# Scores of the late chunks: two fp32 products per head become one stacked fp32r product

## The chip, the cores and the metric

The kernel runs on one core of a Trainium2 chip. The metric is the time of one execution on the device, in microseconds (us). Before the change the median of three runs is 931.97 us, the lowest 931.91 and the highest 932.5. The profile was taken from a further execution of 931.88 us, whose span from the first to the last instruction is 930.1 us.

## The reference, cut to what matters

Two batches of 8 heads with 768 positions of 40 channels go through a gated linear attention (the state of an mLSTM); its output, 1536 tokens of 320 channels, goes through a two-layer network of 2048 hidden channels and then through eight experts of 1024 hidden channels whose weights come from a balanced gate:

```python
C = f_stab[:, :, None, None] * C + i_stab[:, :, None, None] * np.einsum('bhd,bhe->bhde', vt, kt)
n = f_stab[:, :, None] * n + i_stab[:, :, None] * kt
h_tilde = np.einsum('bhde,bhe->bhd', C, qt)          # y = o * h_tilde / max(|n.q|, 1)
...
h = x @ w_in
g = np.maximum(0.01 * h, h)
return (g @ w_out).astype(np.float32)
...
for e in range(E):
    h = np.maximum(x @ w1[e], 0.0)
    out += P[:, e:e + 1] * (h @ w2[e])
```

The kernel computes the recurrence by chunks of 128 tokens. Inside a chunk the scores of a head are the 128 by 128 products of its keys and queries over 40 channels; they are multiplied by a matrix of decays and applied to the values, and a state (`Cst`) carries the rest from chunk to chunk.

## The kernel before, in words

There are 12 chunks. The chunks 0 to 5, and the first 32 steps of the first network (`TABLE = 32`), are issued in a hand-written order, the string `ORDER`, whose words name tasks (`c5.sc` is the scores of chunk 5). Behind the table a loop runs over the steps 32 to 98. A step of this network is `up` (eight matmuls `ha`, L223, 256 columns wide), `leak` and `inner_high` on ScalarE, `inner_low` (`hla`, L723, one subtraction on GpSimd or VectorE) and, three steps later, `down` (six matmuls `ya`, L230 to L232, 320 columns wide). When a run of steps is complete, `empty` adds the sum `ya` into `x` from PSUM (L746, VectorE) or copies it (ScalarE); the next run then reuses the PSUM tiles. Chunks 6 to 11 hang on the steps of this loop by the table of numbers `ATTEND`: the decays of a chunk, its `scores`, its `values`, `recall` and `state`, and its `turn` (the transposes that make `xT`). In the loop the framework's scheduler may interleave what stands in neighbouring tasks; each engine then runs its own instructions strictly in the order in which they are issued.

`scores` (L586 to L592) runs for each head one fp32 matmul with 40 rows of contraction, at partition 0 or 64 by turns. An fp32 matmul shows as two records in the trace, so a chunk has 16 records at L591. `weigh` (L597, VectorE, two instructions) multiplies the scores by the decays and so releases their PSUM tiles.

Other work stands around these places. `decay_mask` (L576) is one GpSimd instruction on 128x1024 numbers; `weigh_keys` (L602) another on 128x320; `spread` (L559, tile `bd`) one on 64x1024. `Cst` (L665) is updated by three VectorE instructions per chunk. The sums of float halves (L259 `rawU`, L315 `rawx`) prepare weights and tokens of the experts; the token turns of the experts (`x0[p].repeat`, `.turn`, `.sums`, steps 36, 54 and 58) copy `x` (L777, `rr`), transpose it on TensorE (L308, `px`) and sum it on VectorE (L315).

What the steps of the loop do in a row:

```python
for g in range(TABLE, NG + LAG):
    up(g); leak(g); inner_high(g); inner_low(g)
    for fn in before[g]: fn()
    down(g - LAG); empty(g - LAG)
    for fn in after[g]: fn()
```

Of the kernel before, what the change touches and what calls it, by code (L numbers as in the profile page):

```python
# [8 lines left out]
F32 = mybir.dt.float32  # L9
F32R = mybir.dt.float32r  # L10
# [4 lines left out]
ALU = mybir.AluOpType  # L15
# [5 lines left out]

ATTEND = ((0, 2, 6, 11, 14), (5, 6, 10, 11, 14), (0, 3, 6, 8, 14), (5, 7, 9, 12, 14))
RUNS = ((0, 0, 8), (1, 0, 12), (0, 8, 16), (1, 12, 16))
MASKED = (0, 1, 2, 3)
VECTORED = ('pl2', 'pl4', 'pu9', 'pu10', 'pu12', 'pl14', 'pl15')
# [18 lines left out]
d15 g17 pl14 h17 u18 pu14 l17 c5.sg pa12 u19 g18 h18 pl13 d16 pb12 g19 l18 d17 h19 l19 u20 pa14 u21 pa13 g20 ph12 pb13  # L46
d18 h20 g21 l20 d19 h21 pb14 ph15 u22 l21 e19 u23 g22 h22 ph13 d20 l22 wl px12 g23 d21 h23 ph14 l23 u24 px14 d22 g24 h24
u25 l24 px15 u26 g25 px13 d23 c5.ou g26 h25 h26 d24 l25 l26 f9 c5.tt@3 u27 c4.tt@1 g27 u28 h27 l27 f7 d25 g28 c5.cr
c4.xi u29 d26 c4.xl g29 h28 h29 d27 l28 l29 u30 e27 u31 g30 c5.xi h30 d28 ws c5.xl c6.bd g31 h31 l30 l31 c4.cr
"""  # L50

F64_SCALE = 2.0 ** -112
# [3 lines left out]
def mlstm_moe_kernel(ctx, tc, qp, q3, kp, kn, vn, gates_in, og, cst_in, scr_in, w_in, w_out, w_gate, w1, w2, out):  # L56
    nc = tc.nc
    B, NCH, P = qp.shape[0:3]
    S = NCH * P
    NT, DM = out.shape  # L60
    D = 40
    DV = D + 1
# [14 lines left out]
    HP = NQ // P  # L77
# [3 lines left out]
    wp = ctx.enter_context(tc.tile_pool(name="wp", bufs=1))  # L81
    x2p = ctx.enter_context(tc.tile_pool(name="x2p", bufs=1))
# [4 lines left out]
    R = B * 32  # L87
    R3 = R + 32
# [3 lines left out]
    bdm = cst[:, P:P + GV]  # L92
# [257 lines left out]
    x2s, X, RRB = {}, {}, [1]  # L350
# [4 lines left out]
    with ExitStack() as st1:  # L355
        ac = st1.enter_context(tc.tile_pool(name="ac", bufs=1))
# [9 lines left out]
        def view(*shape):  # L366
            n = 1
            for x in shape:
                n *= x
            t = R0[:, home[0]:home[0] + n]  # L370
            home[0] += n
            assert home[0] <= R0.shape[1]
            return t.rearrange("p (a b) -> p a b", a=shape[0]) if len(shape) > 1 else t

        sig0 = view(8, DM)
        places = {"kP": view(4, P), "qP": view(4, P), "vt": view(9, DV), "q3": view(G, P), "kn": view(8, D),
                  "Dm": view(8, P), "Pm": view(8, P), "yt": view(8, DV), "dm": view(G, GV)}
        kw = view(9, D)
        sc0 = ac.tile([R3, 2 * S + 512 + 9 * D], F32, tag="sc0", name="sc0")
        sc1 = x2p.tile([R3, 3, S], F32, tag="XT", name="sc1")  # L380
        Ft, It, rst = sc0[0:R, 0:S], sc0[0:R, S:2 * S], sc0[0:R, 2 * S:2 * S + 512]
        ex = sc0[:, 2 * S + 512:].rearrange("p (h d) -> p h d", d=D)
        Mt, G3, T1 = sc1[0:R, 0, :], sc1[:, 1, :], sc1[0:R, 2, :]
        Gt = G3[0:R]


        rawU = ac.tile([P, 7 * UW], F32, tag="rawU", name="rawU")
# [111 lines left out]
        class Chunk:  # L499
# [45 lines left out]
                    nc.sync.dma_start(self.k, kn[self.b, self.s0:self.s0 + P])  # L545

            def load(self):
                self.load_kP()
                self.load_qP()

            def load_rest(self):
                self.load_v()
# [140 lines left out]
        chunks = [Chunk(c) for c in range(NCK)]  # L693
# [40 lines left out]
        def empty(g):  # L734
            j, f = steps[g]
            if (j, f) not in lasts:
                return
            part = sig0[:, 2 * j % 8:2 * j % 8 + 2, :]
            q = 2 * j // (2 * HP)
            if f == NFA - 1 and q not in x2s:  # L740
                x2s[q] = (ac, x2p)[q].tile([P, 2 * HP, DM], F32, tag=("sc0", "XT")[q], name=f"x2_{q}")
            for t in range(2):
                y = yp[j][t]
                o = x2s[q][:, (2 * j + t) % (2 * HP), :] if f == NFA - 1 else part[:, t, :]
                if j in summed:
                    nc.vector.tensor_tensor(o, y, part[:, t, :], op=ALU.add)  # L746
                else:
                    nc.scalar.activation(o, y, AF.Copy)
            summed.add(j)


        before = {g: [] for g in range(NG + LAG)}
        after = {g: [] for g in range(NG + LAG)}
        def attend(c, g_decay, g_scores, g_values, _, g_turn):
            after[g_decay].append(c.decay)
            before[g_scores].append(c.scores)
            after[max(g_scores, g_decay)] += [c.weigh, lambda: c.weigh_keys(nc.gpsimd)]
            before[g_values] += [c.values, c.recall, c.state]
            after[g_values].append(c.attend_all)
            before[g_turn].append(c.turn)  # L760
            if c.ck + 1 < NCK:
                after[g_scores].append(chunks[c.ck + 1].load)
                after[g_values].append(chunks[c.ck + 1].load_rest)

        for j in range(3, NBA):
            g0 = (j - 1) * NFA
            a, b = chunks[2 * j], chunks[2 * j + 1]
            if j > 3:
                after[g0 - 1].insert(0, lambda a=a, b=b: a.spread(b, nc.gpsimd))
            attend(a, *[g0 + x for x in ATTEND[2]])  # L770
            attend(b, *[g0 + x for x in ATTEND[3]])
        after[2 * NFA + 2].append(lambda: load_og(8))
        after[2 * NFA + 8].append(lambda: sigmoid(8))
        g5 = (NBA - 1) * NFA
# [7 lines left out]
        x0, x1 = positions  # L782
        V, GP = nc.vector, nc.gpsimd

        for p, g in enumerate((36, 54, 58)):
            step(g - 1, x0[p].repeat, copy_rest)
            step(g, x0[p].turn, 0, ps_b)
            step(g + 1, x0[p].turn, 1, ps_b)
            step(g + 2, x0[p].sums, V, 0)
            step(g + 3, x0[p].sums, V, 1)  # L790
# [69 lines left out]
        def engine(name):  # L860
            return nc.gpsimd if name in POOLED else nc.vector
# [37 lines left out]
        with tc.manual_schedule():  # L899
            for _ in range(20):  # L900
                nc.tensor.matmul(wps, zero[:, 0:P], zero[:, 0:512], start=True, stop=True)
            for name in ORDER.split():
                name, _, home = name.partition("@")
# [31 lines left out]
    one = cp.tile([1, P], F32, tag="one", name="one")  # L935
# [232 lines left out]
    for it in range(8):  # L1168
        g = 4 + it // 2
# [141 lines left out]
```

## Time and profile before

| | |
|---|---|
| median of three runs | 931.97 us |
| profiled execution | 931.88 us |
| its span | 930.1 us |
| TensorE busy | 924.2 us, 99% |
| VectorE / ScalarE / GpSimd busy | 587.3 / 490.1 / 552.1 us |
| granted TensorE clock, mean | 0.999 |

The engines are called PE (TensorE), PEld (its weight loads), DVE (VectorE), ACT (ScalarE), POOL (GpSimd) and SP (the queue that issues DMAs). PE is busy nearly throughout, so an edit changes the time by what it takes from PE's stream or by what it makes PE wait. A row of the timeline gives start, busy time, engine, line, operation, and in brackets the idle time of that engine before it with what ended it. Records of PE overlap: a matmul's own duration is longer than its distance to the next one, and the distance is what it costs.

### The profile page before, as it was taken

The numbers are of one execution on the slowest core, as the hardware profiler recorded it, in microseconds if no ns is written. First come the engines' busy times: TensorE is split into PE (matmuls) and PEld (weight loads), VectorE is DVE, ScalarE is ACT, GpSimd is POOL, SyncE is SP. The second block draws the span as 40 slices with busy tenths as digits, with TensorE's granted clock in tenths as the row PEclk, the third lists the DMA queues.
The fourth block names the chain that finished last, engine by engine and source line by source line (L and its number), as shares of the span: only waits on it lengthen the run. The fifth ranks groups of instructions, "written<-read, shape, count | busy, mean of one in ns | idle before, by whom it ended". The sixth has DMA issues, their size and how long they took to land.

```text
span 930.1 us, 16892 instructions
## 1 busy us (share of the span) xinstructions
PE 924.2 (99%) x6192; PEld 903.2 (97%) x6192; DVE 587.3 (63%) x1180; ACT 490.1 (53%) x959; POOL 552.1 (59%) x574
## 2 busy tenths in 40 slices
PE   9999999999999999999999999999999999999998
PEld 5899999999999999999999999999999999999998
DVE  8998751523958587666656665665666565666655
ACT  6877445345763645555445445544544455454442
POOL 3330244443442756767777777777777777767762
PEclk9999999999999999999999999999999999999999
DMA  8773131110301110111111111111111111111002
GB/s 273 253 233 129 34 111 31 56 39 3 88 14 33 52 38 24 52 38 38 37 38 53 46 52 38 37 38 38 50 48 50 41 38 38 38 49 49 30 2 85
DMA packets 57384, 56.49 MB, mean 61 GB/s; under 512 B 7654, under 2 KB 48086, under 8 KB 57302
## 3 DMA queue, kind: packets, MB, share of 16 engines
q1 hardware_dynamic: 57302, 55.43, 19.7%
q8 instruction: 48, 0.79, 0.4%
q14 instruction: 34, 0.28, 0.1%
HBM read 53.43 MB, written 1.97 MB: 60 GB/s over the span
## 4 chain that ended last, share of the span: by engine, by line
PE 94%; DVE 3%; ACT 1%; DMA 1%; issue 1%; SPq 0%; ACTq 0%; DVEq 0%
PE y L230 12%; PE y L231 12%; PE y L232 12%; PE ha L223 9%; PE b L1030 8%; PE b L1031 8%; PE b L1033 8%; PE b L1032 8%; PE ya L230 3%; PE ya L232 3%; PE ya L231 3%; PE yps L607 2%; PE sps L591 1%; PE zps L613 1%; PE dps L619 1%
## 5 line engine op out<-in xcount | busy, mean ns | idle before, releaser
L1054 POOL TENSOR_TENSOR hl<-c,hh 128x384 fp32r<-128x384 f32 x192 | 197.3, 1028 | 180.2 <-ACT c L1053 155.5
L230 PE MATMUL y<-w_e,hh 128*128 128x320 f32 x768 | 238.6, 311 | 0.0
L231 PE MATMUL y<-w_e,hh 128*128 128x320 f32 x768 | 237.0, 309 | 0.0
L232 PE MATMUL y<-w_e,hl 128*128 128x320 f32 x768 | 236.9, 308 | 0.0
L1112 DVE SCALAR_TENSOR_TENSOR acc<-y,Pg,acc 128x320 f32<-128x320 f32 x336 | 179.1, 548 | 63.4 <-PE y L232 56.3
L1052 ACT ACTIVATE hh<-c 128x384 fp32r<-128x384 f32 x192 | 99.8, 520 | 208.5 <-DVE c L1049 208.5
L1030 PE MATMUL b<-X,w_e 128*128 128x384 f32 x448 | 152.7, 341 | 0.2 <-DVE s L1070 0.2
L1031 PE MATMUL b<-X,w_e 128*128 128x384 f32 x448 | 151.0, 337 | 0.0
L1033 PE MATMUL b<-X,w_e 96*128 96x384 f32 x448 | 151.0, 337 | 0.0
L1032 PE MATMUL b<-X,w_e 128*128 128x384 f32 x448 | 150.9, 337 | 0.0
L230 PEld LDWEIGHTS y<-w_e,hh 128*128 128x128 f32 x768 | 144.3, 188 | 1.7 <-DVE acc L1110 1.1
L231 PEld LDWEIGHTS y<-w_e,hh 128*128 128x128 f32 x768 | 144.3, 188 | 0.0
L232 PEld LDWEIGHTS y<-w_e,hl 128*128 128x128 f32 x768 | 144.2, 188 | 0.0
L1053 ACT ACTIVATE c<-c 128x384 f32<-128x384 f32 x192 | 101.0, 526 | 18.0 <-ACT hh L1052 0.7
L1049 DVE TENSOR_TENSOR c<-b,s 128x384 f32<-128x384 f32 x192 | 100.6, 550 | 13.4 <-PE b L1033 10.0
L223 PE MATMUL ha<-xT,w_a 128*128 128x256 f32 x768 | 107.8, 285 | 0.0
L223 PEld LDWEIGHTS ha<-xT,w_a 128*128 128x128 f32 x768 | 100.1, 190 | 1.1 <-ACT gg L712 0.2
L1077 DVE SCALAR_TENSOR_TENSOR hl<-b,hh 128x384 fp32r<-128x384 f32 x64 | 35.6, 557 | 95.4 <-ACT hh L1076 95.4
L723 POOL TENSOR_TENSOR hla<-gg,hha 128x256 fp32r<-128x256 f32 x64 | 49.3, 772 | 70.3 <-ACT hha L718 62.4
L259 POOL TENSOR_TENSOR raw_e<-raw_e 128x256 f32<-128x256 f32 x116 | 85.2, 743 | 4.5
L1030 PEld LDWEIGHTS b<-X,w_e 128*128 128x128 f32 x448 | 84.8, 189 | 1.3 <-DVE s L1070 0.6
L1031 PEld LDWEIGHTS b<-X,w_e 128*128 128x128 f32 x448 | 85.3, 190 | 0.0
(200 smaller groups left out, 1496.7 us busy)
## 6 DMA issues: line engine op xcount, KB each, us to landing
raw_e<-in_w_dram SPq DMA_DIRECT2D x31, 320.0 KB, 2.9
raw_e<-in_w_dram SPq DMA_DIRECT2D x62, 128.0 KB, 2.2
raw_e<-in_w_dram SPq DMA_DIRECT2D x248, 32.0 KB, 1.9
raws<-in_w_in_dram SPq DMA_DIRECT2D x8, 768.0 KB, 5.9
rawU<-in_w_out_dram SPq DMA_DIRECT2D x4, 640.0 KB, 5.6
R<-in_kp_dram SPq DMA_DIRECT2D x10, 256.0 KB, 3.4
R<-in_qp_dram SPq DMA_DIRECT2D x10, 256.0 KB, 3.6
raws<-in_w_out_dram SPq DMA_DIRECT2D x4, 640.0 KB, 4.6
```

The lines of the kernel that those rows point to most:

```text
L223: nc.tensor.matmul(h_ps, t1[:, ws, c * P:(c + 1) * P], xt[:, xs, t0:t0 + n], start=(j == 0), stop=(j == len(MM1) - 1),)
L230: nc.tensor.matmul(y_ps, a, t2[:, c, :], start=first, stop=False)
L231: nc.tensor.matmul(y_ps, a, t2[:, 2 + c, :], start=False, stop=False)
L232: nc.tensor.matmul(y_ps, b, t2[:, c, :], start=False, stop=last)
L1030: nc.tensor.matmul(bank, f[:, 0], b[:, 0], start=fresh, stop=False, skip_group_check=not fresh)
L1031: nc.tensor.matmul(bank, f[:, 0], b[:, 2], start=False, stop=False, skip_group_check=not fresh)
L1032: nc.tensor.matmul(bank, f[:, 2], b[:, 0], start=False, stop=False, skip_group_check=not fresh)
L1033: nc.tensor.matmul(bank, f[0:K3, 1], b[0:K3, 1], start=False, stop=True, skip_group_check=not fresh)
L1049: nc.vector.tensor_tensor(c, part, plus, op=ALU.add)
L1053: nc.scalar.activation(c, c, AF.Relu)
L1054: nc.gpsimd.tensor_tensor(hl[a][b], c, hh[a][b].bitcast(F32), op=ALU.subtract)
L1112: nc.vector.scalar_tensor_tensor(out=o, in0=y, scalar=Pg[:, 2 * HP * q + t, e:e + 1], in1=o, op0=ALU.mult, op1=ALU.add)
```

## The change: what it does

For chunks 6 to 11 `load` now brings each 40-row block of keys and queries three times, one under the other, into 120 partitions (six DMAs in place of two per chunk). `stack(n)` turns the keys (n = 0) and the queries (n = 1) of a chunk into a stack of fp32r numbers: for each half of the heads a CAST writes the rounded part of 120x512 numbers, and a SCALAR_TENSOR_TENSOR with two inputs in SBUF (the rounded part and the plain numbers) writes either the rounded part or the remainder, by a column of zeros and ones. These are eight new VectorE instructions per chunk. `scores_stacked` then runs one fp32r matmul per head, 120 rows deep, which sums the three products of rounded parts and remainders.

The stacks live in two of the three `raw` buffers until the scores of chunk 11. So the token turns 1 and 2 of expert 0, which need such buffers, stand at steps 72 and 74 in place of 54 and 58. The table's end gets the loads and both stacks of chunk 6. Two rows and one column of `ATTEND` that nothing reads are dropped.

```diff
-g31 h31 l30 l31 c4.cr
+g31 h31 l30 l31 c4.cr c6.ld c6.s0 c6.s1
...
             def load(self):
-                self.load_kP()
-                self.load_qP()
+                if self.ck == 10:
+                    second_half()
+                for t, src in zip(plain, (kp, qp)):
+                    src = src[self.b, self.c].rearrange("(i p) j t -> p i (j t)", i=2)[0:D]
+                    for r in range(3):
+                        nc.sync.dma_start(t[r * D:(r + 1) * D].rearrange("p (i m) -> p i m", i=2), src)
+
+            def stack(self, n):
+
+                if len(stacks) == n:
+                    stacks.append(wp.tile([GW, 12 * P], F32R, tag="raw", name=f"stack{n}", bufs=3))
+                t, x = stacks[n], plain[n]
+                one = bdm[0:GW, (n + 1) * DV:(n + 1) * DV + 1]
+                for i in range(2):
+                    s = slice(4 * i * P, 4 * (i + 1) * P)
+                    high = t[:, 8 * P:12 * P]
+                    nc.vector.tensor_copy(high, x[:, s])
+                    nc.vector.scalar_tensor_tensor(out=t[:, s], in0=high.bitcast(F32), scalar=one, in1=x[:, s],
+                                                   op0=ALU.mult, op1=ALU.subtract)
+
+            def scores_stacked(self):
+                self.sps = self.bank("sc")
+                for i in range(2):
+                    for j in range(4):
+                        t = slice((4 * i + j) * P, (4 * i + j + 1) * P)
+                        nc.tensor.matmul(self.sps[i][:, j, :], stacks[0][:, t], stacks[1][:, t], start=True, stop=True)
...
-        def attend(c, g_decay, g_scores, g_values, _, g_turn):
+        def attend(c, g_decay, g_scores, g_values, g_turn):
             after[g_decay].append(c.decay)
-            before[g_scores].append(c.scores)
+            before[g_scores].append(c.scores_stacked)
...
             if c.ck + 1 < NCK:
-                after[g_scores].append(chunks[c.ck + 1].load)
-                after[g_values].append(chunks[c.ck + 1].load_rest)
+                n = chunks[c.ck + 1]
+                after[g_scores].append(lambda: n.stack(0))
+                after[g_scores + 1].append(lambda: n.stack(1))
+                after[g_values].append(n.load_rest)
+            if c.ck + 2 < NCK:
+                after[g_scores + 1].append(chunks[c.ck + 2].load)
...
-        for p, g in enumerate((36, 54, 58)):
+        for p, g in enumerate((36, 72, 74)):
...
-        chunks[6].load()
         chunks[6].load_rest()
+        chunks[7].load()
```

The order in which VectorE works at chunk 6's scores, before the change (`x_0<-ya_12` is the sum that releases the PSUM tiles for the next run, `sps_6` the scores):

```order
L663 TENSOR_TENSOR R_76<-dps_668,cst 120x369
L259 TENSOR_TENSOR rawU<-rawU 128x256
L665 SCALAR_TENSOR_TENSOR Cst_106<-Cst_106,decC,R_76 120x123 x3
L259 TENSOR_TENSOR rawU<-rawU 128x256
L746 TENSOR_TENSOR x_0_1361<-ya_12_0_1378,R_76 128x320
L746 TENSOR_TENSOR x_0_1361<-ya_12_1_1379,R_76 128x320
L597 TENSOR_TENSOR R_76<-sps_6_1497,R_76 128x4x128
L597 TENSOR_TENSOR R_76<-sps_6_1498,R_76 128x4x128
```

And the same place in the changed kernel, from the update of `Cst` on:

```order
L699 SCALAR_TENSOR_TENSOR Cst_106<-Cst_106,decC,R_76 120x123 x3
L574 CAST stack_1409<-sc_96 120x512
L259 TENSOR_TENSOR rawU<-rawU 128x256
L575 SCALAR_TENSOR_TENSOR stack_1409<-stack_1409,cst,sc_96 120x512
L259 TENSOR_TENSOR rawU<-rawU 128x256
L574 CAST stack_1409<-sc_96 120x512
L259 TENSOR_TENSOR rawU<-rawU 128x256
L575 SCALAR_TENSOR_TENSOR stack_1409<-stack_1409,cst,sc_96 120x512
L574 CAST stack_1414<-R_76 120x512
L780 TENSOR_TENSOR x_0_1361<-ya_12_0_1378,R_76 128x320
L575 SCALAR_TENSOR_TENSOR stack_1414<-stack_1414,cst,R_76 120x512
L780 TENSOR_TENSOR x_0_1361<-ya_12_1_1379,R_76 128x320
```

Eight instructions now stand between the last update of `Cst` and the first sum into `x_0`, where one stood; three sums of `rawU` moved behind `Cst` (the other two stood some rows further up), and the second half of the queries' stack follows behind these rows.

TensorE at the same place in the changed kernel (`ya_0` are the PSUM tiles that the sums into `x_0` release; before, all eight score matmuls stood between the first and the second row, and the eight `ha` of one step were together):

```order
L223 MATMUL ha_1502<-xT_1318,w_a_415 128x256 x8
L230 MATMUL ya_0_0_1527<-w_a_302,hha_1440 128x320
L231 MATMUL ya_0_0_1527<-w_a_302,hha_1440 128x320
L232 MATMUL ya_0_0_1527<-w_a_302,hla_1441 128x320
L223 MATMUL ha_1545<-xT_1318,w_a_555 128x256
L583 MATMUL sps_6_1517<-stack_1414,stack_1409 128x128 x4
L230 MATMUL ya_0_1_1528<-w_a_302,hha_1440 128x320
L231 MATMUL ya_0_1_1528<-w_a_302,hha_1440 128x320
L232 MATMUL ya_0_1_1528<-w_a_302,hla_1441 128x320
L223 MATMUL ha_1545<-xT_1318,w_a_555 128x256 x4
L583 MATMUL sps_6_1518<-stack_1414,stack_1409 128x128 x4
```

The scores are split into two halves of four, and half the sums `ya` moved ahead of each.

VectorE between the weighing of chunk 6 and the scores of chunk 7 in the changed kernel (`rr_1` and `rawx_0` are the token turn at step 36, `zps`, `yps` and `dps` chunk 6's values, recall and state):

```order
L631 TENSOR_TENSOR R_76<-sps_6_1518,R_76 128x4x128
L574 CAST stack_1409<-sc_96 120x512
L575 SCALAR_TENSOR_TENSOR stack_1409<-stack_1409,cst,sc_96 120x512
L574 CAST stack_1409<-sc_96 120x512
L575 SCALAR_TENSOR_TENSOR stack_1409<-stack_1409,cst,sc_96 120x512
L815 COPY rr_1_2686<-x_0_1361 128x256 x2
L315 TENSOR_TENSOR rawx_0_1576<-rawx_0_1576 128x256 x4
L658 TENSOR_TENSOR R_76<-zps_1641,decT 128x328
L574 CAST stack_1414<-R_76 120x512
L663 TENSOR_TENSOR R_76<-yps_1632,R_76 128x328
L575 SCALAR_TENSOR_TENSOR stack_1414<-stack_1414,cst,R_76 120x512
L668 TENSOR_SCALAR den_1657<-R_76 128x8
```

The keys' stack of chunk 7 stands ahead of the copies and the queries' stack among chunk 6's values, and the four sums of `rawx` now follow one another; behind these rows come the second half of the queries' stack, the updates of `Cst` and the weighing of chunk 7.

## Rows read from the trace of the kernel before

**Rows 1.** The page: busy time and share of the span; the chain that ended last.

```profile
PE 924.2 (99%) x6192; PEld 903.2 (97%) x6192; DVE 587.3 (63%) x1180; ACT 490.1 (53%) x959; POOL 552.1 (59%) x574
...
PE 94%; DVE 3%; ACT 1%; DMA 1%; issue 1%; SPq 0%; ACTq 0%; DVEq 0%
```

**Rows 2.** Timeline of PE around chunk 11's scores: start us, busy us, then the instruction.

```profile
208.17 1.12 PE L223 MATMUL ha<-xT,w_a 128*128 128x256 f32 x8
209.22 1.16 PE L591 MATMUL sps<-R 40*128 40x128 f32 x16
...
210.56 0.31 PE L231 MATMUL ya<-w_a,hha 128*128 128x320 f32 x1
...
211.29 1.12 PE L223 MATMUL ha<-xT,w_a 128*128 128x256 f32 x8
212.25 0.31 PE L230 MATMUL ya<-w_a,hha 128*128 128x320 f32 x1
212.40 0.31 PE L231 MATMUL ya<-w_a,hha 128*128 128x320 f32 x1
```

**Rows 3.** Groups by line and shape, 95 to 225 us: count, busy us, mean ns.

```profile
L607 PE MATMUL yps<-R 128*128 128x41 f32 x96 | 11.4, 278 | 0.1
...
L441 DVE SCALAR_TENSOR_TENSOR mv<-mv,rco,sc 64x384 f32<-64x384 f32 x1 | 0.6, 599 | 0.0
```

**Rows 4.** Timeline of PE at the scores of chunks 6 and 7.

```profile
113.35 1.12 PE L223 MATMUL ha<-xT,w_a 128*128 128x256 f32 x8
...
122.63 1.87 PE L607 MATMUL yps<-R 128*128 128x41 f32 x16
...
127.90 0.94 PE L591 MATMUL sps<-R 40*128 40x128 f32 x12
```

**Rows 5.** Timeline of DVE in the same stretch.

```profile
109.28 0.41 DVE L259 TENSOR_TENSOR rawU<-rawU 128x256 f32<-128x256 f32 x1
109.61 1.73 DVE L665 SCALAR_TENSOR_TENSOR Cst<-Cst,decC,R 120x123 f32<-120x123 f32 x3
111.26 0.41 DVE L259 TENSOR_TENSOR rawU<-rawU 128x256 f32<-128x256 f32 x1
113.11 0.93 DVE L746 TENSOR_TENSOR x<-ya,R 128x320 f32<-128x320 f32 x2 [1.44 <-PE ya L232]
...
121.69 0.49 DVE L777 COPY rr<-x 128x256 f32<-128x256 f32 x2 [4.74 <-PE px L308]
125.53 0.50 DVE L624 TENSOR_TENSOR R<-zps,decT 128x328 f32<-128x328 f32 x1 [3.34 <-PE zps L613]
```

**Rows 6.** Timeline of POOL in the same stretch.

```profile
110.04 1.17 POOL L576 TENSOR_SCALAR_AFFINE_SELECT R<-R 128x1024 f32<-128x1024 f32 x1 [42.60 <-PE ha L223]
111.17 1.10 POOL L723 TENSOR_TENSOR hla<-gg,hha 128x256 fp32r<-128x256 f32 x1
112.23 0.74 POOL L602 TENSOR_TENSOR R<-R 128x320 f32<-128x320 f32 x1
112.93 1.44 POOL L723 TENSOR_TENSOR hla<-gg,hha 128x256 fp32r<-128x256 f32 x2
115.41 0.73 POOL L723 TENSOR_TENSOR hla<-gg,hha 128x256 fp32r<-128x256 f32 x1 [1.04 <-ACT hha L718]
122.39 0.73 POOL L723 TENSOR_TENSOR hla<-gg,hha 128x256 fp32r<-128x256 f32 x1 [6.25 <-ACT hha L718]
123.08 1.89 POOL L559 TENSOR_TENSOR bd<-mv,rco 64x1024 fp32r<-64x1024 f32 x1
...
125.98 1.32 POOL L576 TENSOR_SCALAR_AFFINE_SELECT R<-R 128x1024 f32<-128x1024 f32 x1
```

**Rows 7.** Two lines by themselves, whole span: ns shortest/median/longest.

```profile
L665 DVE SCALAR_TENSOR_TENSOR Cst<-Cst,decC,R x24: 294/342/1212, 34.5 to 178.8; 120x123 f32<-120x123 f32 x24
...
L777 DVE COPY rr<-x x10: 281/284/662, 105.3 to 254.5; 128x256 f32<-128x256 f32 x10
```

**Rows 8.** Windows: PE, PEld, DVE, ACT, POOL busy us, PEclk, DMA share, GB/s.

```profile
140.00:222.00 82.00, 82.00 (x666) 80.59 (x665) 23.90 (x60) 36.03 (x86) 34.52 (x44) 1.00 0.12 36
```

More of the change, by code (lines that the diff above doesn't have):

```diff
@@ L19 @@
 NEG = -1.0e30
-ATTEND = ((0, 2, 6, 11, 14), (5, 6, 10, 11, 14), (0, 3, 6, 8, 14), (5, 7, 9, 12, 14))
+ATTEND = ((0, 3, 6, 14), (5, 7, 9, 14))
 RUNS = ((0, 0, 8), (1, 0, 12), (0, 8, 16), (1, 12, 16))
@@ L48 @@
 u25 l24 px15 u26 g25 px13 d23 c5.ou g26 h25 h26 d24 l25 l26 f9 c5.tt@3 u27 c4.tt@1 g27 u28 h27 l27 f7 d25 g28 c5.cr
-c4.xi u29 d26 c4.xl g29 h28 h29 d27 l28 l29 u30 e27 u31 g30 c5.xi h30 d28 ws c5.xl c6.bd g31 h31 l30 l31 c4.cr
+c4.xi u29 d26 c4.xl g29 h28 h29 d27 l28 l29 u30 e27 u31 g30 c5.xi h30 d28 ws c5.xl c6.bd g31 h31 l30 l31 c4.cr c6.ld c6.s0 c6.s1
 """
@@ L375, in mlstm_moe_kernel @@
         sig0 = view(8, DM)
-        places = {"kP": view(4, P), "qP": view(4, P), "vt": view(9, DV), "q3": view(G, P), "kn": view(8, D),
+        both = view(8, P)
+        places = {"kP": both[:, 0:4], "qP": both[:, 4:8], "vt": view(9, DV), "q3": view(G, P), "kn": view(8, D),
                   "Dm": view(8, P), "Pm": view(8, P), "yt": view(8, DV), "dm": view(G, GV)}
@@ L379, in mlstm_moe_kernel, with second_half @@
         sc0 = ac.tile([R3, 2 * S + 512 + 9 * D], F32, tag="sc0", name="sc0")
-        sc1 = x2p.tile([R3, 3, S], F32, tag="XT", name="sc1")
+        sc1 = x2p.tile([P, 3, S], F32, tag="XT", name="sc1")
         Ft, It, rst = sc0[0:R, 0:S], sc0[0:R, S:2 * S], sc0[0:R, 2 * S:2 * S + 512]
         ex = sc0[:, 2 * S + 512:].rearrange("p (h d) -> p h d", d=D)
-        Mt, G3, T1 = sc1[0:R, 0, :], sc1[:, 1, :], sc1[0:R, 2, :]
+        Mt, G3, T1 = sc1[0:R, 0, :], sc1[0:R3, 1, :], sc1[0:R, 2, :]
         Gt = G3[0:R]
+        plain = [sc1.rearrange("p a s -> p (a s)")[0:GW, 0:8 * P], both[0:GW].rearrange("p h t -> p (h t)")]
+        stacks = []
+        def second_half():
+            t = x2p.tile([P, 3 * S], F32, tag="XT", name="x2_1")
+            x2s[1] = t[:, 0:2 * HP * DM].rearrange("p (t d) -> p t d", d=DM)
+            o = (2 * HP - 2) * DM
+            plain[0] = t[0:GW, o:o + 8 * P]
         rawU = ac.tile([P, 7 * UW], F32, tag="rawU", name="rawU")
@@ L740, in empty @@
             if f == NFA - 1 and q not in x2s:
-                x2s[q] = (ac, x2p)[q].tile([P, 2 * HP, DM], F32, tag=("sc0", "XT")[q], name=f"x2_{q}")
+                x2s[q] = ac.tile([P, 2 * HP, DM], F32, tag="sc0", name=f"x2_{q}")
             for t in range(2):
@@ L769, in mlstm_moe_kernel @@
                 after[g0 - 1].insert(0, lambda a=a, b=b: a.spread(b, nc.gpsimd))
-            attend(a, *[g0 + x for x in ATTEND[2]])
-            attend(b, *[g0 + x for x in ATTEND[3]])
+            for c, times in ((a, ATTEND[0]), (b, ATTEND[1])):
+                attend(c, *[g0 + x for x in times])
         after[2 * NFA + 2].append(lambda: load_og(8))
@@ L887, in mlstm_moe_kernel @@
         tasks["c6.bd"] = lambda: chunks[6].spread(chunks[7], engine("c6.bd"))
+        tasks["c6.ld"] = chunks[6].load
+        for n in range(2):
+            tasks[f"c6.s{n}"] = lambda n=n: chunks[6].stack(n)
         for n in range(2 * NUA):
```

## The prediction

> **What bounds the kernel now.** I read the page first, then PE's timeline where the edited matmuls stand, then the timelines of DVE and POOL beside them. PE is busy 924.2 of 930.1 us and makes 94% of the chain that ended last [rows 1], so the sum goes by PE: what leaves its stream is gained, and each time it waits is lost, since nothing later in the program stands still to absorb it. The reader should see in [rows 2] that a step without scores and one with scores differ by a whole block, and in [rows 5, 6] that DVE and POOL, though far from full, delay each other whenever they work side by side. The resolution that I use throughout is 0.2%, 1.9 us. The profiled execution took 931.88 us and the median is 931.97, so I sum against the former, and the 0.1 us between them is inside the rounding.
>
> **What PE's stream loses.** In a step without scores the second `ya` starts 1.11 us after the first `ha` (211.29 to 212.40); with chunk 11's scores it takes 2.39 us (208.17 to 210.56) [rows 2]. The scores cost 1.28 us per chunk. They become eight records. No row before shows an fp32r matmul with 128 columns, so I bound it. From below: `ha` has 256 columns and goes at 0.96/8 = 0.120 us each (211.29 to 212.25), `ya` 320 columns at 0.15 (212.25 to 212.40) [rows 2]; 0.027 to 0.03 us per 64 columns leads to about 0.063 us at 128, 0.50 per chunk, and 0.78 saved. From above: if fp32r at this width took two records as fp32 does, 16 records by the pitch of `yps`, (1.87 - 0.28)/15 = 0.106 us [rows 3, 4], make 1.70 us, and 0.42 is lost. The nearest row is `yps`: it streams only 41 columns per record and still cannot go faster than 0.106, and it loads 128 columns of 4-byte weights as the new matmul does. I take 0.11, so 0.88 per chunk. Saved: 0.40 per chunk, 2.4 us over six chunks; ends -4.7 and +2.5.
>
> The Trainium skill, "TensorE: Matmul & The Clock Gate", section "Back-to-back issue gap", gives 81 ns as the sustained distance of matmuls with their weight loads at 128 columns. By that figure the block would be 0.65 us and the saving 3.8 us, an estimate; no run here shows it.
>
> **What DVE gains, and what hides it.** Eight instructions per chunk come in. The scalar_tensor_tensor has no row at 512 columns: 384 columns took 0.60 us [rows 3] and 123 take 0.34 [rows 7], so 0.73 at 512, some 0.66 between starts. The cast lies between the copy of 256 columns (0.28, [rows 7]), which gives 0.35 at best, and the other instruction's 0.66; I take 0.40. A chunk's stacks are 4 x 0.66 + 4 x 0.40 = 4.2 us, 25 us for all. From 140 to 222 us DVE is busy 23.9 of 82 and PE never idle [rows 8]; chunks 8 to 11 put in about 17 us, and the moved token turns (two, by the same rows two copies, four sums each, some 5 us with waits) fall there too. That cover is wide, so I cost both at nothing; if a stack still came late, it would cost that chunk its 0.4 us gain first. The extra DMAs (four more per chunk on SP) for chunks 8 to 11 are issued a whole chunk ahead; for chunk 6 they stand before `rawU`'s loads, whose sums have moved later as well. The two tight places are chunk 6 and chunk 7.
>
> **The lock.** Three `Cst` updates with both inputs in SBUF took 1.73 us from 109.61, where three medians are 1.03; the longest single one is 1.21 us [rows 5, 7]. It ran beside POOL's affine_select of 110.04 to 111.21 and ended 0.13 us after that, so of its own 0.34 us 0.2 lay under POOL's end. POOL's next `hla` then took 1.10 us to 112.27 instead of the 0.72 to 0.74 of the others [rows 6]: its own 0.73 starts at 111.54, 0.13 before DVE's sum of 111.26 was over [rows 5]. By turns, each waits for nearly the whole instruction of the other. The sums that read PSUM (113.11, 0.93 for two) ran beside POOL's `hla` of 112.93 and neither lost anything. A copy too goes from 0.28 up to 0.66 [rows 7].
>
> The Trainium skill, "SBUF — State Buffer", section "Who interferes with whom", says that a DVE instruction with two SBUF inputs, or a copy or cast in a two-port mode, and a GpSimd instruction that reads SBUF exclude one another for the full instruction. The rows just read agree, at 1.21 us against 0.34. It is the rule that speaks against this change, because all eight new instructions are of these two kinds.
>
> **Chunk 6.** PE wants `ya_0` when its eight `ha` of 113.35 are through, at 113.35 + 0.96 = 114.31 [rows 2, 4]. That tile is free only after the sum `x_0<-ya_12_0` (half of 0.93). Three sums `rawU`, 0.33 apart (109.28 to 109.61), no longer stand ahead of the `Cst` updates, so these end near 109.6. Then come three casts, three sums and two scalar_tensor_tensor: 3 x 0.40 + 3 x 0.33 + 2 x 0.66 = 3.5 us, to 113.1, and the sum into `x_0` to 113.55. Alone, DVE is 0.8 us early and chunk 6 costs nothing. But from 110.04 on POOL has six instructions in a row, 1.17 + 1.10 + 0.74 + 1.44 + 0.73 less the 0.37 that one lost, 4.8 us [rows 6]; at 110.04 DVE has one cast and one sum behind it and six left (2.8 us). Taking turns, with some 0.16 us of overlap at each of 12 handovers (0.2 and 0.13 above), they are through at 110.04 + 4.8 + 2.8 - 1.9 = 115.7, the sum into `x_0` at 116.2: PE waits 1.9 us. The two halves of the scores then follow DVE closely, some 0.3 us more. I take 2.2; the ends are 0 (DVE goes first, or casts do not lock) and 3.6 (no overlap).
>
> **Chunk 7.** Here DVE used to be idle before the values, 4.74 and 3.34 us [rows 5]. The keys' stack fits into the first gap. The queries' stack stands behind `zps`, which comes at 125.53, with four casts and products among `yps`, `den` and `dps`; PE wants `sps_7` at 127.90 [rows 4], and POOL works at the same time (`bd` 1.89, affine_select 1.32, `hla` [rows 6]). Without the lock the first half is ready near 127.4 and the second near 129.0, both in time. With three or four turns lost to POOL at 0.7 to 1.0 each, less what moves forward on POOL, the second half is 0 to 3 us late. I take 1.0.
>
> Sum: 931.9 - 2.4 + 2.2 + 1.0 = 932.7; I forecast **932.7 us**, no change that can be told.
>
> **Rivals.** *Stacks in time*: POOL's instructions start later than DVE's, or the casts are not locked, and the two places cost together 0 to 0.6. For it: the 0.8 us of slack alone and DVE's 1.44 us of idle time at chunk 6 [rows 5]; against it the 1.73 us row. Time 931.9 - 2.4 + 0 to 0.6 = 929.5 to 930.1.
>
> *The lock through chunk 7*: each of the four stack instructions behind `zps` waits for one of POOL's, 4 x 0.9 = 3.6 us on the half that PE takes last. With chunk 6's 2.2 it gives 931.9 - 2.4 + 5.8 = 935.3, slower. It decides from the point at which the two waits together pass 4.3 us. For it speaks that `den`'s neighbours there already ran beside POOL's 1.32 us affine_select [rows 6]; against it that POOL's `hla` in front of it came only after 6.25 us of idling and might run earlier.
>
> *Records at the stream's rate*, 0.063 us: -4.7, which is 927.2 without waits and 930.4 with my 3.2 us of them. Against it: 41 columns at 0.106.
>
> *Two records per matmul*: +2.5 and 3.2, so 937.6. Against it: `ha` and `ya`, which are fp32r, go at one column per pass.
>
> **How the numbers follow.** My forecast 0.42 (own range 931.0 to 935.0: faster 0.02, same 0.28, slower 0.12); stacks in time 0.30 (faster 0.28, same 0.02); lock through chunk 7 0.13 (same 0.01, slower 0.12); stream rate 0.10 (faster 0.06, same 0.04); two records 0.05 (slower). That is faster 0.36, same 0.35, slower 0.29. The range 928.8 to 937.0 leaves out the lower half of the stream-rate case, and the two-record case.
>
> **What would show it.** Eight records per chunk at 0.10 to 0.12 us, in two groups of four, confirm the saving; 0.06 or 0.21 would overturn it. At chunk 6 PE should idle 1.5 to 2.5 us before the first `ya_0`, ended by DVE's sum into `x`, with casts or products of 0.7 to 1.5 us on DVE beside POOL. At chunk 7 a wait of some 1 us before the second half of `sps_7`, ended by DVE's stack. Between 140 and 222 us PE should not idle; if it does, the cover of chunks 8 to 11 was wrong. I am wrong if chunk 6 shows no wait.

## The result and the profile after

The changed kernel takes **938.37 us** (median of four runs, 936.56 to 939.42) where the kernel before took 931.94 us in the same comparison; the ratio is 1.0063 [1.0051, 1.0075]. It is slower, and it lies above the range of the prediction. The profiled execution is the shortest of the four, 936.56 us with a span of 934.8 us, against 931.88 us before; by itself it would lie just inside the range. One execution of all is left out of the numbers: one of the kernel with the sums of `rawU` later (below) took 2328.45 us.

The page after answers to [rows 1]: PE is busy for almost the same time and keeps its 94% of the chain that ended last; DVE's share of the chain rises from 3 to 4%.

```profile
PE 923.5 (99%) x6141; PEld 903.9 (97%) x6144; DVE 624.0 (67%) x1228; ACT 492.0 (53%) x959; POOL 556.9 (60%) x574
...
PE 94%; DVE 4%; issue 1%; ACT 1%; DMA 0%; SPq 0%; DVEq 0%; ACTq 0%
```

The timeline of PE after, at the scores of chunks 6, 7 and 11 (it answers to [rows 2, 4]):

```profile
113.42 1.12 PE L223 MATMUL ha<-xT,w_a 128*128 128x256 f32 x8
117.57 0.41 PE L230 MATMUL ya<-w_a,hha 128*128 128x320 f32 x1 [3.04 <-DVE x L780]
...
118.23 0.66 PE L583 MATMUL sps<-stack,stack 120*128 120x128 f32 x4
...
129.85 1.11 PE L223 MATMUL ha<-xT,w_a 128*128 128x256 f32 x8
132.81 0.64 PE L583 MATMUL sps<-stack,stack 120*128 120x128 f32 x4 [1.85 <-DVE den L668]
...
134.83 0.95 PE L583 MATMUL sps<-stack,stack 120*128 120x128 f32 x4
135.57 1.75 PE L223 MATMUL ha<-xT,w_a 128*128 128x256 f32 x8
...
211.24 1.12 PE L223 MATMUL ha<-xT,w_a 128*128 128x256 f32 x8
212.20 1.01 PE L583 MATMUL sps<-stack,stack 120*128 120x128 f32 x8
213.05 0.36 PE L230 MATMUL ya<-w_a,hha 128*128 128x320 f32 x1
213.25 0.30 PE L231 MATMUL ya<-w_a,hha 128*128 128x320 f32 x1
```

Three things are to be seen. At chunk 11 the second `ya` stands 2.01 us after the first `ha` instead of 2.39, so the saving is there: 0.38 us, and over the step boundaries of all six chunks I read 0.39 each, 2.35 us in all. At chunks 6 and 7 PE stands still for 3.04 and 1.85 us (and for 0.11 us before the second half of chunk 6's scores). (The second wait carries the name of `den`; the stack that the matmul reads was written by the scalar_tensor_tensor of 131.92, which ended 0.15 us before the matmul.) And behind the second wait the same instructions take longer: eight `ha` 1.75 us instead of 1.11, four score records 0.95 instead of 0.64. The windows say why. Their columns are the busy times of PE, PEld, DVE, ACT and POOL, then the granted clock:

```profile
132.00:133.00 1.00, 0.19 (x2) 0.22 (x3) 1.00 (x4) 0.00 (x0) 0.00 (x0) 1.00 0.00 0
133.00:134.00 1.00, 1.00 (x7) 1.00 (x7) 1.00 (x5) 0.00 (x0) 0.00 (x0) 0.72 0.00 0
134.00:135.00 1.00, 1.00 (x6) 0.99 (x5) 1.00 (x4) 0.00 (x0) 0.29 (x1) 0.50 0.00 0
135.00:136.00 1.00, 1.00 (x7) 1.00 (x6) 1.00 (x2) 0.00 (x0) 1.00 (x2) 0.50 0.42 100
136.00:137.00 1.00, 1.00 (x7) 1.00 (x7) 1.00 (x2) 0.00 (x0) 0.17 (x1) 0.57 0.65 222
137.00:138.00 1.00, 1.00 (x9) 1.00 (x8) 1.00 (x3) 0.55 (x2) 0.00 (x0) 1.00 0.93 267
...
140.00:222.00 82.00, 82.00 (x650) 81.63 (x649) 41.73 (x89) 35.40 (x84) 36.62 (x45) 1.00 0.22 59
```

PE is busy in every row from 133 on, but the granted clock fell to 0.50 (1.2 instead of 2.4 GHz) soon after PE had stood still, and came back 3.4 us later. That lost some 1.7 us, half of the stretch. Busy time does not show it; the clock column does. The last row answers to [rows 8]: DVE has 41.7 us of work there instead of 23.9, and PE never waits.

DVE after, at chunk 6 and then ahead of chunk 7 (it answers to [rows 5]):

```profile
110.23 0.42 DVE L574 CAST stack<-sc 120x512 fp32r<-120x512 f32 x1
110.57 0.42 DVE L259 TENSOR_TENSOR rawU<-rawU 128x256 f32<-128x256 f32 x1
110.90 1.58 DVE L575 SCALAR_TENSOR_TENSOR stack<-stack,cst,sc 120x512 fp32r<-120x512 f32 x1
112.41 0.96 DVE L259 TENSOR_TENSOR rawU<-rawU 128x256 f32<-128x256 f32 x1
113.29 0.96 DVE L574 CAST stack<-sc 120x512 fp32r<-120x512 f32 x1
114.17 0.95 DVE L259 TENSOR_TENSOR rawU<-rawU 128x256 f32<-128x256 f32 x1
115.04 1.21 DVE L575 SCALAR_TENSOR_TENSOR stack<-stack,cst,sc 120x512 fp32r<-120x512 f32 x1
116.17 0.94 DVE L574 CAST stack<-R 120x512 fp32r<-120x512 f32 x1
117.04 0.48 DVE L780 TENSOR_TENSOR x<-ya,R 128x320 f32<-128x320 f32 x1
...
118.50 0.41 DVE L574 CAST stack<-R 120x512 fp32r<-120x512 f32 x1
...
119.17 0.74 DVE L575 SCALAR_TENSOR_TENSOR stack<-stack,cst,R 120x512 fp32r<-120x512 f32 x1
...
125.13 3.06 DVE L815 COPY rr<-x 128x256 f32<-128x256 f32 x2 [0.98 <-PE px L308]
128.11 2.75 DVE L315 TENSOR_TENSOR rawx<-rawx 128x256 f32<-128x256 f32 x4
```

POOL in the same stretch (it answers to [rows 6]):

```profile
110.10 1.84 POOL L610 TENSOR_SCALAR_AFFINE_SELECT R<-R 128x1024 f32<-128x1024 f32 x1 [42.42 <-PE ha L223]
111.91 1.18 POOL L757 TENSOR_TENSOR hla<-gg,hha 128x256 fp32r<-128x256 f32 x1
113.04 0.92 POOL L636 TENSOR_TENSOR R<-R 128x320 f32<-128x320 f32 x1
113.93 2.90 POOL L757 TENSOR_TENSOR hla<-gg,hha 128x256 fp32r<-128x256 f32 x3
...
125.04 1.89 POOL L593 TENSOR_TENSOR bd<-mv,rco 64x1024 fp32r<-64x1024 f32 x1
126.89 1.14 POOL L610 TENSOR_SCALAR_AFFINE_SELECT R<-R 128x1024 f32<-128x1024 f32 x1
```

A cast that POOL leaves alone takes 0.41 us, beside POOL 0.94 to 0.96; a scalar_tensor_tensor 0.74 against up to 1.58. The engines take turns from 110.1 until POOL's last `hla` ends at 116.83. From 117 on, with POOL idle, the same instructions run at their own length. Further down, two copies that took 0.49 us before begin 0.09 us behind `bd` and take 3.06 us, until POOL's affine_select is over.

### The profile page after: what moved, and what is told of

Same layout as the page of the kernel before. It is cut to its first block, busy times and chain, and to the rows that moved or that the text cites. A ratio compares the mean times of both kernels' runs of the same rounds, so it can differ in the third digit from the quotient of the medians.

```text
span 934.8 us, 16876 instructions
## 1 busy us (share of the span) xinstructions
PE 923.5 (99%) x6141; PEld 903.9 (97%) x6144; DVE 624.0 (67%) x1228; ACT 492.0 (53%) x959; POOL 556.9 (60%) x574
## 4 chain that ended last, share of the span: by engine, by line
PE 94%; DVE 4%; issue 1%; ACT 1%; DMA 0%; SPq 0%; DVEq 0%; ACTq 0%
PE y L230 12%; PE y L231 12%; PE y L232 12%; PE ha L223 9%; PE b L1071 8%; PE b L1072 8%; PE b L1074 8%; PE b L1073 8%; PE ya L230 3%; PE ya L232 3%; PE ya L231 3%; PE yps L641 2%; PE zps L647 1%; PE sps L583 1%; PE px L308 1%
## 5 line engine op out<-in xcount | busy, mean ns | idle before, releaser
L757 POOL TENSOR_TENSOR hla<-gg,hha 128x256 fp32r<-128x256 f32 x64 | 52.3, 819 | 68.0 <-ACT hha L752 55.7
```

## The experiments

My theory after reading the two traces: (a) DVE and POOL lock each other out at chunks 6 and 7 and the stacks come late; (b) a wait of PE costs more than itself, through the clock. The rivals: DVE's own load makes the stacks late; the moved token turns cost something; the stacked product saves less than it seems; the longer matmuls come from something other than the wait. Each kernel is timed beside the kernel before on the same chip.

**The turns alone.** The kernel before with its token turns at the new steps.

```diff
-        for p, g in enumerate((36, 54, 58)):
+        for p, g in enumerate((36, 72, 74)):
```

> The kernel before with one part of the change alone: the token turns 1 and 2 of expert 0 at steps 72 and 74 instead of 54 and 58. Theory (the loss lies at chunks 6 and 7, between 113 and 137 us): 932.0 us, within 0.4 of before, no wait of TensorE over 0.4 us between 200 and 260 us. Rival (the moved turns collide with VectorE's backlog at 230 to 258 us): 0.8 to 1.5 us slower than before.

Measured 932.1 us against 932.07, ratio 1.0000 [0.9992, 1.0009]. The moved turns cost nothing.

**Chunk 6 as before.** Chunks 7 to 11 stay stacked.

```diff
-            before[g_scores].append(c.scores_stacked)
+            before[g_scores].append(c.scores if c.ck < 7 else c.scores_stacked)
```

> The changed kernel with chunk 6 back on eight fp32 score matmuls; chunks 7 to 11 stacked, their loads one chunk later where they share a buffer with chunk 6. Theory: chunk 6's wait of 3.0 us goes, and because VectorE is then free at 117 to 121 us and chunk 7's stacks are done before its values, chunk 7's wait and the fall of the clock go too; what stays is the saving of five chunks at 0.39 us: 930.0 us, range 929.6 to 931.0. Rival (chunk 7 waits for its own stacks whatever chunk 6 does): wait of 1.5 us or more before its scores and granted clock under 0.999, 933.4 us.

Measured 932.06 us where 930.0 was expected, ratio 1.0008 [0.9994, 1.0021]: most of the loss is gone, but the expected gain did not come. Ten of the twelve runs took 930.65 to 933.05 us; the other two took 937.4 us at a mean granted clock of 0.994, so this kernel too can lose several us to the clock. In the profile neither chunk's scores wait. In their place `zps` waited 1.15 us at 125.7 for ACT, whose exponentials had moved. And chunk 7's key loads, whose buffer is free early, moved up to the program's start, among the loads of the tables; PE waited 0.86 us at 24.9 there, and the clock was at half from 28.0 to 31.4 us in the profiled execution.

**Chunks 6 and 7 as before.**

```diff
+            before[g_scores].append(c.scores if c.ck < 8 else c.scores_stacked)
```

> The changed kernel with chunks 6 and 7 on eight fp32 score matmuls each; chunks 8 to 11 stacked. Theory: no wait of TensorE between 110 and 230 us, granted clock 0.999, saving of four chunks at 0.39 us: 930.4 us, range 930.0 to 930.9. Rival (the late chunks' stacks on VectorE or the moved turns also cost something): 931.5 us or more.

Measured 931.76 us, ratio 0.9995 [0.9987, 1.0004]. From 110 to 230 us of the span PE never waits for more than 0.2 us, the clock is full, and this stretch is 1.52 us shorter than before, four chunks at 0.38 to 0.39, as the theory had it. So the stacked product does save. But the time is the rival's: in the profile 0.9 us are lost by 32 us of the span and 1.3 us by 45 us, and chunk 8's key loads now stand at 16 us. Windows of this kernel (first row) and a row of PE's timeline (second):

```profile
20.00:30.00 10.00, 9.17 (x67) 6.29 (x63) 9.35 (x18) 8.19 (x12) 4.71 (x3) 1.00 1.01 290
```

```profile
25.86 0.41 PE L335 MATMUL pt_a<-cst,R 128*128 128x128 f32 x2 [0.83 <-DVE R L681]
```

The DMA share, the number after the clock, is 1.01 there; the wait was 0.17 us before.

**The casts on ScalarE.**

```diff
-                    nc.vector.tensor_copy(high, x[:, s])
+                    nc.scalar.activation(high, x[:, s], AF.Copy)
```

> The changed kernel with the four casts of each chunk's stacks on ScalarE instead of VectorE. Theory (VectorE and GpSimd exclude one another, so each instruction taken from VectorE also takes one turn of waiting): at chunk 6 three turns fewer but six instructions left against GpSimd's five, wait about 2.6 us; at chunk 7 the copies still stand behind GpSimd's spread, wait about 1.0 us; 934.5 us, range 932.8 to 936.0. Rival (VectorE is simply overloaded, its own busy time counts): wait of chunk 6 down by the casts' own 1.2 us to 1.8, chunk 7 near 0.4, no fall of the clock, 932.3 us.

Measured 938.8 us, ratio 1.0076 [1.0064, 1.0088], no gain where 934.5 (up to 936.0) was expected. Chunk 6's waits were 1.78 + 0.79 us, close to the expected 2.6, but chunk 7's were 1.61 + 0.95. DVE and ACT now wait for each other over the one scratch tile for the rounded part:

```profile
116.35 0.63 ACT L574 ACTIVATE stack<-R 120x512 fp32r<-120x512 f32 x1 [2.27 <-DVE stack L575]
```

The clock was at half for 3.4 us behind chunk 6's waits and 6.8 us behind chunk 7's, so this kernel loses 5.1 us to the clock alone. I had left the clock out of this expectation too.

**PE kept busy.** 24 matmuls whose result nothing reads stand before chunk 6's scores and 14 before chunk 7's, in the places of the waits.

```diff
-            before[g_scores].append(c.scores_stacked)
+            if c.ck < 8:
+                before[g_scores].append(lambda: c.keep_busy({6: 24, 7: 14}[c.ck]))
+                after[g_scores].append(c.scores_stacked)
```

> The changed kernel with 24 and 14 matmuls more on TensorE (256 columns, 2.9 and 1.7 us, their results overwritten) just before the places where it waits at chunks 6 and 7; the scores of both chunks stand six matmuls ya later, which costs some 0.6 us. Theory (the clock falls because TensorE stood idle, and that is the 3 to 4 us that the two waits themselves don't explain): the waits are filled with work of the same length, the granted clock stays at 0.999, runs agree within 1 us, and the time is 935.5 us (934.8 to 936.3), some 3 us better than the changed kernel although work was added. Rival (the clock falls for another reason, or hardly counts): clock again 0.995 to 0.998, runs 3 us apart, 938 to 939 us.

Measured 937.29 us, ratio 1.0052 [1.0040, 1.0064], where 935.5 was expected; the runs lie 3.7 us apart where 1 was expected. PE's timeline and the windows:

```profile
115.63 3.04 PE L581 MATMUL sps<-xT,w_a 128*128 128x256 f32 x24
...
132.69 1.84 PE L581 MATMUL sps<-xT,w_a 128*128 128x256 f32 x14
...
140.49 1.76 PE L648 MATMUL yps<-R 128*128 128x41 f32 x14 [0.74 <-DVE R L638]
```

```profile
113.00:118.00 5.00, 5.00 (x42) 5.00 (x42) 5.00 (x6) 1.73 (x5) 5.00 (x6) 1.00 0.13 36
...
129.00:135.00 6.00, 6.00 (x51) 6.00 (x51) 6.00 (x10) 3.23 (x4) 3.02 (x4) 1.00 0.19 53
...
143.00:146.00 3.00, 3.00 (x15) 3.00 (x15) 2.93 (x9) 0.00 (x0) 0.00 (x0) 0.50 0.49 166
```

With the waits filled, the clock stays at 1.00 past chunks 6 and 7 (until 142.7); waits of 0.19 to 0.35 us are left at chunk 6. The stacks are as late as before, so the time is not won back. A new wait of 0.28 and 0.74 us came before chunk 7's `yps`, since VectorE's order had changed, and half clock followed that one. In three of the six runs the mean granted clock was 1.0; these took 936.02, 936.05 and 936.62 us, near the expected 935.5. None of the four runs of the change itself had a clock above 0.998.

**`hla` of steps 32 to 35 on VectorE**, which takes POOL's small products out of chunk 6's stretch and gives DVE more to do.

```diff
-            (nc.vector if g < TABLE else nc.gpsimd).tensor_tensor(hl, h_ps.pop(g), hh.bitcast(F32), op=ALU.subtract)
+            (nc.vector if g < TABLE + 4 else nc.gpsimd).tensor_tensor(hl, h_ps.pop(g), hh.bitcast(F32), op=ALU.subtract)
```

> The changed kernel with the subtractions hla of the steps 32 to 35 on VectorE instead of GpSimd, so VectorE gets four instructions of 0.33 us more at chunk 6 and GpSimd four fewer. Theory (the two engines exclude one another): the wait at chunk 6 falls from 3.0 to some 2.2 us, because VectorE waits for two GpSimd instructions instead of five; 937.3 us. Rival (VectorE is slow there by its own load): three more instructions ahead of the sum into x, the wait grows to some 4.0 us and the time to 939.5.

```profile
111.37 0.42 DVE L574 CAST stack<-sc 120x512 fp32r<-120x512 f32 x1
...
117.09 0.48 DVE L780 TENSOR_TENSOR x<-ya,R 128x320 f32<-128x320 f32 x1
```

```profile
117.22 0.66 PE L583 MATMUL sps<-stack,stack 120*128 120x128 f32 x4 [1.07 <-DVE stack L575]
```

DVE has more work and chunk 6 is *less* late, 1.07 us instead of 3.04. From the first cast to the first sum into `x` DVE now runs ten instructions in 5.72 us (111.37 to 117.09), where it ran eight in 6.81 us (110.23 to 117.04): it was the lock and not DVE's load. That accounts for 1.1 us of the fall; the rest comes from TensorE's order, where four more `ha` and the first half of the scores now stand ahead of `ya_0`. Chunk 7 still waits (2.66 us), with 6.8 us at half clock behind it, and the time is 936.85 us (937.3 expected), ratio 1.0047 [1.0034, 1.0060].

**The sums of `rawU` later.** DVE is relieved of the sums among chunk 6's stacks.

```diff
-            step(63 + k, experts[0].sums, V, (k,))
+            step(63 + k, sums_behind, k)
...
+            with tc.issue_after(chunks[8].weighed.ins):
+                experts[0].sums(V, (k,))
```

> The changed kernel with the four sums of rawU issued behind the weighing of chunk 8, so that three instructions of 0.33 us leave the row of VectorE at chunk 6; the order on TensorE then puts the first half of chunk 6's scores before ya_0. Theory (the two engines exclude one another): each of the five stack instructions left ahead of that half still waits for one of GpSimd's, wait of TensorE at chunk 6 together 2.0 to 2.8 us; chunk 7 as before, 938 us. Rival (own load): casts and products alone end at 114.0 us, no wait over 0.3 us at chunk 6; 935 us.

```profile
117.28 1.06 PE L583 MATMUL sps<-stack,stack 120*128 120x128 f32 x4 [2.27 <-DVE stack L575]
```

DVE has 1 us less to do by itself and chunk 6 still waits 2.27 us, again the lock. Other steps became late (0.99 and 1.10 us at chunk 7, 0.86 and 0.97 us later), and the time is 940.18 us where 938 was expected (three runs, 938.31 to 942.19), ratio 1.0084 [1.0069, 1.0098].

**The stacks fitted into the plan.** Chunk 6's scores two steps later, its second stack in step 34, the sums of the token turn pinned behind.

```diff
+            for c, times in ((a, ATTEND[0] if j > 3 else (0, 6, 8, 14)), (b, ATTEND[1] if j > 3 else (7, 9, 11, 14))):
...
+        after[34].append(second_stack)
```

> The changed kernel with the stacks fitted to what VectorE can do beside GpSimd: rawU's sums behind chunk 8's weighing, the queries' stack of chunk 6 behind the sums into x, chunk 6's scores at step 38 and its values at 40, chunk 7's decays, scores and values at 39, 41 and 43, both stacks of chunk 7 right behind chunk 6's scores, the token turns' copies and sums behind the weighing. Theory (the loss is only these two places): no wait over 0.3 us, granted clock 0.999, and the six chunks' saving of 2.35 us stays: 929.8 us, range 929.4 to 930.6. Rival (the stacks cost TensorE time wherever they stand): a wait of 1 us or more at chunk 6 or 7, 932 us or more.

Measured 935.42 us where 929.8 was expected, ratio 1.0032 [1.0020, 1.0044]. Chunk 6 no longer waits, but a cast for chunk 7 met POOL's `bd`:

```profile
127.94 3.04 DVE L574 CAST stack<-R 120x512 fp32r<-120x512 f32 x1
```

That half of chunk 7's scores was 1.04 us late, and three later steps 0.87 to 1.16 us. Placing the stacks by hand moved the waits and did not remove them.

**`bd` on VectorE.** The product ahead of chunk 7's two copies goes from POOL to DVE.

```diff
-                after[g0 - 1].insert(0, lambda a=a, b=b: a.spread(b, nc.gpsimd))
+                after[g0 - 1].insert(0, lambda a=a, b=b, j=j: a.spread(b, nc.vector if j == 4 else nc.gpsimd))
```

> The changed kernel with the decay's bd product before chunk 7's copies on VectorE (64x1024, about 1.1 us) instead of GpSimd. Theory: the two copies of x took 3.06 us because they shared the port with bd and the affine_select, so they fall to 0.5 to 1.0 each, the stacks of chunk 7 come some 1 us sooner even with bd's 1.1 us on VectorE, chunk 7's wait falls from 1.85 to 0.3 to 1.0 us and the half clock behind it may go: 935 to 937.5 us. Rival: chunk 7 is late by VectorE's own load, then bd adds its 1.1 us to the wait: 2.9 us there, 939.5 us. Chunk 6's wait is the same for both, 3.0 us.

Measured 934.96 us, ratio 1.0032 [1.0020, 1.0044]. DVE and PE of this kernel:

```profile
126.05 1.47 DVE L593 TENSOR_TENSOR bd<-mv,rco 64x1024 fp32r<-64x1024 f32 x1 [1.35 <-PE aps L600]
...
128.67 0.81 DVE L815 COPY rr<-x 128x256 f32<-128x256 f32 x1
...
129.74 0.28 DVE L815 COPY rr<-x 128x256 f32<-128x256 f32 x1
```

```profile
117.62 0.42 PE L230 MATMUL ya<-w_a,hha 128*128 128x320 f32 x1 [3.03 <-DVE x L780]
...
133.99 0.64 PE L583 MATMUL sps<-stack,stack 120*128 120x128 f32 x4 [0.64 <-DVE den L669]
```

The copies fall from 3.06 to 1.09 us for the two, DVE does 1.47 us more, and chunk 7's wait goes from 1.85 to 0.64: what made it late was that the copies stood behind `bd` on the port. Chunk 6 is as it was. Here the half clock followed chunk 6's wait, and none came behind chunk 7's:

```profile
118.00:119.00 1.00, 1.00 (x10) 0.93 (x9) 1.00 (x4) 0.00 (x0) 0.00 (x0) 1.00 0.66 229
...
120.00:121.00 1.00, 1.00 (x6) 0.99 (x5) 0.56 (x1) 0.00 (x0) 0.00 (x0) 0.50 0.08 12
```

**Chunks 8 to 11 stacked, chunk 8's keys loaded later.** This is the kernel with chunks 6 and 7 as before, with chunk 8's key loads queued behind chunk 7's query load.

```diff
+            with tc.issue_after(chunks[7].came.ins):
+                n.load()
```

> Chunks 6 and 7 with the six matmuls, 8 to 11 stacked, and chunk 8's key load queued behind chunk 7's query load (it stood at the start, among the tables' loads, in the run before with chunks 6 and 7 as before). Theory: that early load cost what the stacked chunks saved. Then the start is the kernel before's, nothing waits later, and four chunks save 4 x 0.39 = 1.6 us: 930.5 us, 0.998 of before. Rival: the start's 0.9 to 1.3 us was chance of one profile or has another cause, and the saving is lost elsewhere: 931.8 us, as in the run before.

> The same kernel as the earlier run with chunks 6 and 7 as before, chunk 8's keys loaded at the start, for a comparison on the same chip. Theory (the early load costs it): 931.8 us again, with TensorE's wait at 25 us of the span and some 1.3 us more than the run with the later load. Rival (chance): the two agree within 0.4 us.

With the later load 930.64 us, ratio 0.9988 [0.9979, 0.9997], shorter than the kernel before by 1.3 us, which is less than the 1.9 us that the prediction took as its resolution; the same kernel with the early load 931.25 us, ratio 0.9995 [0.9986, 1.0003], much as in its first run. The expected 1.56 us of saving lies in the first interval (0.3 to 2.0 us) and not in the second (up to 1.3 us). DMA's share from 20 to 30 us is 0.86 again, as before, against 1.01 and 0.97. The two kernels differ by 0.6 us, between the 1.3 of the theory and the 0.4 of the rival. The profiles do not show that the early load costs this: in its second profile PE has no wait at 25 us and reaches the same row (`pt_a`, L335) at 43.88 us where the kernel before is at 43.87, and the two profiled executions took 930.99 us with the later load and 931.05 with the early one. So the medians favour the later load by little; that the early load is what costs is not shown.

## Why the prediction was wrong

**One sum fits the losses from 35 us on.** Taken per profiled execution: 0.39 us saved per stacked chunk, plus PE's waits between 35 and 230 us that the kernel before does not have, plus half of the time at half clock, all in us.

| kernel | saved | waits | clock | sum | measured |
|---|---|---|---|---|---|
| the change | -2.35 | 5.00 | 1.7 | +4.4 | +4.7 |
| casts on ScalarE | -2.35 | 5.1 | 5.1 | +7.9 | +7.7 |
| `hla` on VectorE | -2.35 | 4.4 | 3.4 | +5.5 | +5.5 |
| `bd` on VectorE | -2.35 | 3.7 | 1.7 | +3.0 | +3.1 |
| sums later | -2.35 | 6.2 | 3.4 | +7.3 | +7.8 |
| fitted | -2.35 | 4.1 | 1.7 | +3.5 | +4.0 |
| chunks 8 to 11, late keys | -1.56 | 0.2 | 0 | -1.3 | -0.9 |

Measured is the profiled execution less the kernel before (its profiled execution for the first row, its median on the same chip for the others). What remains is up to 0.5 us; executions of the kernel before differ by 0.8 us or more on one chip. The sum does not cover what is lost before 35 us: the first run of chunks 6 and 7 as before would come to -1.4 where -0.1 was measured. The kernel with PE kept busy is not in the table because work was added to it.

**The clock: the step that failed.** The prediction summed two waits at their own length and had no term for the clock: it put that cost at nothing without a reason. The waits themselves came to 5.0 us where it had 3.2, which gives 934.5; in the profiled execution one stretch at half clock adds 1.7 us. The other three executions of the change took 1.4 to 2.9 us longer, at a mean granted clock of 0.995 to 0.996 instead of 0.998; a second such stretch would lower the mean by 1.7 / 935 = 0.002 and add 1.7 us, so most of them probably had two, though no profile of them was kept. With two the sum is +6.1, and the median measured +6.4, which puts it above the range. That the half clock comes from the waits is shown in two ways: with the waits filled it stayed away from chunk 7, and in all thirteen profiles no stretch at half clock begins elsewhere than at the end of a wait of 0.74 us or more or up to 2.3 us behind it.

**Chunk 6: right mechanism, term too small.** 2.2 was forecast, 3.04 and 0.11 measured; the experiments with `hla` and with `rawU` both confirm the lock. My sum had the `Cst` updates end near 109.6, and let POOL's affine_select run first at its own 1.17 us. The updates ended at 110.3, and the affine_select took 1.84, since DVE's cast and sum of 110.23 and 110.57 went ahead of it undelayed. That is 0.67 us, and the rest is mostly the overlap at a handover: the row of DVE that begins at 110.90 ended 0.54 us behind the affine_select, of its own 0.66 between starts, so 0.12 us lay under it where I had put 0.16 twelve times.

**Chunk 7: right mechanism in the wrong place.** I looked for turns lost among the four stack instructions behind `zps` and took 1.0 us, 0 to 3. The stack instructions there took 0.41 and 0.74 us, alone. What was late was ahead of them: two copies of 0.49 us together [rows 5], which my sum for chunk 7 did not name, stood behind `bd`, and the sums of `rawx` and `zps` behind them. The copies had stood at 121.69 [rows 5], 1.4 us before `bd` of 1.89 us [rows 6]; I moved neither against the other. A change that delays PE by 3 us at chunk 6 also moves those engines against each other.

**The rival with the right sign.** The lock through chunk 7 was to decide once the two waits together passed 4.3 us; they came to 5.0, and without the clock its sum of 935.3 would have been near. I gave it 0.13. But its mechanism did not occur: the four stack instructions behind `zps` ran undelayed, and only its total was near, by luck.

**What held.** Eight records, (213.05 - 212.20)/8 = 0.106 us apart at chunk 11 where I took 0.11; 0.39 us saved per chunk for 0.40; scalar_tensor_tensor 0.74 for 0.73; cast 0.41, some 0.33 between starts, where 0.40 went into the sum; no wait from 140 to 222 us; the moved turns at nothing. The rivals at the stream's rate and at two records are refuted. That I took 0.11 rightly was in part luck: the fp32 score records before, also 128 columns wide but with 40 rows at partition 0 or 64 by turns, came 16 in 1.16 us [rows 2], at most 0.073 us each, and I did not weigh that row against `yps`. The rule of the Trainium skill ("SBUF — State Buffer", "Who interferes with whom") on the shared port held for casts, copies and scalar_tensor_tensor alike, up to 3.06 us for two copies of 0.28.

**What stays open.** Chunk 6's wait of 3.04 us was not followed by half clock in the profile of the change, and one of 3.03 us was in that of `bd` on VectorE, with the same instructions around it. From 20 to 230 us the profiles have twenty places with a wait of 0.6 us or more (waits less than 2 us apart taken as one place), and half clock followed nine of them: six of the seven with 1.6 us or more, three of the thirteen with 0.64 to 1.16 us. No run tells what decides it.

## What to carry to other kernels

When PE is the bound, price a wait of PE at its length and put beside it, as a case of its own with a chance, a stretch at half clock, here 1.7 us and sometimes twice that: it followed six of the seven longest waits and few of the short ones; and look at the granted clock before explaining longer matmuls by anything else. When VectorE gets new copies, casts or two-input instructions, lay them against GpSimd's timeline, also where an old copy merely shifts next to a long GpSimd instruction. The late, well covered chunks took the change without a wait and the first two did not, so apply such an edit where the cover is, and check where its loads are issued.

## What was new about the hardware

- Behind nine waits of PE, of 0.74 to 3.03 us, the granted clock was at half for 3.4 or 6.8 us, in the changed kernel from 133.4 to 136.9; behind eleven others, of 0.64 to 3.04 us, it stayed full. At half clock the eight `ha` took 1.75 us instead of 1.11.
- DVE and POOL alternate almost instruction by instruction: six instructions of POOL, 4.8 us by themselves, took 6.73 us beside eight of DVE, and each side waited for the other, but for DVE's first two, which ran at their own length while POOL waited.
- fp32r records with 128 columns and weights of 120 rows come every 0.106 us, as do `yps` records with 41 columns [rows 4].
